# Interleaving the first two chunks of an FFT-and-MLP kernel, and moving the conversion of its second weight matrix

## The chip, the cores and the metric

The kernel runs on one core of one Trainium2 chip. The metric is the device time of one execution in microseconds (us). The engines are TensorE (PE, matrix products; PEld is its weight load), VectorE (DVE), ScalarE (ACT), GpSimd (POOL) and SyncE (SP, which issues most DMAs). Each engine runs its instructions in order; they wait for each other by semaphores.

## The reference

```python
def _attn_ref(x):                       # x: 8 x 3136 x 256
    X = np.fft.fft(x, axis=1)
    X = np.fft.fft(X, axis=2)
    return X.real.astype(np.float32)

def _moe_ref(x, g_ln, w_ch1, w_ch2):    # w_ch1: 256 x 1024, w_ch2: 1024 x 256
    mu = np.mean(x, axis=-1, keepdims=True)
    var = np.mean((x - mu) ** 2, axis=-1, keepdims=True)
    xn = (x - mu) / np.sqrt(var + 1e-06) * g_ln
    ch = np.maximum(xn @ w_ch1, 0.0) @ w_ch2
    return (x + ch).astype(np.float32)
```

The weights arrive as 64-bit floats, and the kernel converts them itself.

## The kernel before

**Stages.** The DFT over the 3136 rows of each of the 8 batches is split in two. `step1(b, i)` makes the inner transform of two of 14 row slices; its result goes to DRAM (`store1`) and comes back in another layout (`relayout`, tile `s2`). `step2(m, part)` makes the outer one for pair `m` of frequency groups (8 pairs for each batch, m counts over all). Its result in PSUM (`ps2`, one bank with the tag "fft" and one with the tag "y") is copied out as chunks of 256 tokens: `ckh` and `ckl`, a rounded part and the rest of it ("h" and "l" of `part`), and `ck`, the whole ("f").

**The MLP.** Every product in float32 is made as three products of rounded parts (`PASSES`). Only half of the frequencies is computed: a sum and a difference of two halves, `pa` and `pb`, give a token and its mirror. The work of a chunk is eight tiles, one for each 128 hidden features `f`. `s` numbers the tiles over all chunks: before, `c, f = divmod(s, 8)`. For a tile, `moe1_a(s)` is the first product (6 matmuls into `ab`, two buffers), ScalarE's copy `asb` and VectorE's two halves of `h`; `moe1_b(s)` is ScalarE's `h_hi` (ReLU and rounding) and VectorE's `h_lo`; `moe2(s)` is the second product, 12 matmuls into `acc`. `acc` of chunk c has the two banks of the tag `acc{c % 2}`. A first product can start only when `h` of the tile two before is made, since that empties its `ab`.

**Residual and end of a chunk.** `residual(c, i)` makes the reference's x again for 128 tokens (4 matmuls for both i, tile `psy`), before in the two banks of the other parity, `acc{(c + 1) % 2}`; `residual_e` (ScalarE, `ye`) and `residual_y` (VectorE, `y`, mean and variance) follow. `std` (ScalarE) and `inverse_std` (VectorE, `ve`, `r`) give the factor, `finish(c, i)` (VectorE, `o`) adds both parts, which empties `acc`; `store_out` writes.

**Weights.** Each quarter of w1 and of w2 is converted by `convert_z` (ScalarE, `ew`), `convert_m` (VectorE, `mw`, `fw`), `convert_b` (VectorE, `ew` twice) and, for w2, `finish_w2` (VectorE, `fw`). `split_w2` gives `w_hi` on ScalarE and `w_lo` on POOL. w1 is also transformed (`transform_w1`), rounded and its rest kept (`rest_w1`, `rest_w1_copy`: `w_lo`), in halves k: k=0 for f up to 3, k=1 from f=4. Quarter n of w2 serves f = 2n and 2n + 1.

**Order.** The order of PE, ACT, DVE and POOL is that in which the code is written; for SP too in the first part. A hand-written start runs to tile 5. Then a loop over s issues, for each step s: `moe1_b(s - 1)`, `moe1_a(s)`, the list `late[s]`, `moe2(s - 3)`, the list `after[s]`. `add_late` and `add` fill the lists: here stand the residuals, the ends of chunks, step1, step2 and the folds of later batches on POOL.

Of the kernel before, what the change touches and what calls it, by code (L numbers as in the profile page):

```python
# [146 lines left out]
def tile_kernel(ctx: ExitStack, tc: tile.TileContext, x, g_ln, w1, w2, tu, tab, tz, ty, tw, out):  # L147
# [192 lines left out]
    hh = {}  # L340

    def moe1_a(s, passes=((0, 1), (1, 0), (0, 0))):
        c, f = divmod(s, 8)
        w = width(c)
# [51 lines left out]
    def moe2(s, halves=((0, 0), (0, 1), (1, 0), (1, 1))):  # L396

        c, f = divmod(s, 8)
        hs = hh[s]
# [102 lines left out]
    def convert_a(key, wp):  # L502
        convert_m(key, wp)
        convert_z(key, wp)
# [181 lines left out]
    with tc.manual_schedule(engines={E.PE, E.Activation, E.DVE, E.Pool}):  # L686
        with tc.manual_schedule(engines={E.SP}):
# [61 lines left out]
            relayout(0, 0, 2)  # L749
            relayout(0, 2, 4)  # L750
            relayout(0, 4, 8)
            nc.sync.dma_start(tab_s[:, :, gb[4]:gb[8]], tab[:, :, gb[4]:gb[8]])
            load_w2(2)
            relayout(0, 8, 16)
# [9 lines left out]
            for i in range(NU):  # L764
# [31 lines left out]
            step2(1, "f")  # L796
            convert_a("w2_2", w2p[2])
            step2(1, "hl", 1)
            moe2(0)
            moe1_b(3)  # L800
            moe1_a(4)
            convert_b("w2_2")
            f = finish_w2(2)
            nc.gpsimd.tensor_scalar(out=neg, in0=ty_s[:, 1, 129:130], scalar1=2.0, scalar2=-1.0,
                                    op0=ALU.mult, op1=ALU.add)
            moe2(1)
            step2(2, "m")
            moe1_b(4)
            split_w2(2, f)
            moe1_a(5)  # L810
            step2(2, "hf")
            step2(2, "l")
            convert_a("w2_3", w2p[3])
# [41 lines left out]
```

## Time and profile before

| | us |
|---|---|
| median of 3 runs | 988.58 (988.18 to 991.56) |
| the profiled execution | 988.67 |
| its span | 986.9 |
| granted TensorE clock | 1.00 |

| engine | busy us | share of the span |
|---|---|---|
| PE | 976.8 | 99% |
| DVE | 815.5 | 83% |
| ACT | 535.6 | 54% |
| POOL | 252.1 | 26% |

The profile gives times in us from the span's start. A row of a timeline has start, duration, engine, line, operation, tiles written and read, and in brackets how long the engine stood idle before it and what ended that. Matmuls are pipelined: the duration of one is longer than the distance to the next. The chain is the work that ended last, followed back; its shares tell what the span consists of.

### The profile page before, as it was taken

Reading aid. Unit: us, or ns where it says so; the run is one execution under the profiler, and the core shown is the slowest. Engines: PE = TensorE matmul, PEld = TensorE weight load, DVE = VectorE, ACT = ScalarE, POOL = GpSimd, SP = SyncE. Lnnn points to the kernel's source line nnn. Section 1 sums busy time; section 2 is a strip of 40 time slices with the busy share of each in tenths; the row PEclk is TensorE's granted clock in tenths of the full one; section 3 lists DMA queues with packets and bytes.
Section 4 is the critical chain, followed back from the end, with each engine's and each line's share of the span. In section 5 each row is a group of like instructions: output and inputs, shape, how many; then the busy total and the mean of one; then the engine's idle time right before and its main releaser. Section 6 shows DMA issues by size and latency. Waiting matters only on the chain.

```text
span 986.9 us, 22042 instructions
## 1 busy us (share of the span) xinstructions
PE 976.8 (99%) x8426; PEld 962.9 (98%) x8427; DVE 815.5 (83%) x2190; ACT 535.6 (54%) x1416; POOL 252.1 (26%) x282
## 2 busy tenths in 40 slices
PE   9899999999999999999999999999999999999998
PEld 6699999999999999999999999999999999999998
DVE  6888887888888888878888888888888888888887
ACT  3655655555555555555555556555555554555553
POOL 3247343224322332322342234223322300000000
PEclk9999999999999999999999999999999999999999
DMA  8924352215221252112521242212311112100101
GB/s 336 330 101 134 101 173 76 87 54 150 76 97 55 75 161 87 65 65 73 164 86 54 86 139 87 96 55 75 109 52 36 54 53 88 44 23 22 44 23 44
DMA packets 41161, 92.12 MB, mean 93 GB/s; under 512 B 4080, under 2 KB 18400, under 8 KB 40160
## 3 DMA queue, kind: packets, MB, share of 16 engines
q1 hardware_dynamic: 39088, 87.25, 26.7%
q0 software_dynamic: 736, 2.47, 0.7%
q8 instruction: 67, 1.10, 0.5%
q10 hardware_dynamic: 1232, 0.99, 0.3%
q14 instruction: 38, 0.31, 0.1%
HBM read 50.32 MB, written 40.37 MB: 92 GB/s over the span
## 4 chain that ended last, share of the span: by engine, by line
PE 91%; DVE 7%; ACT 2%; issue 1%; ACTq 0%; DVEq 0%
PE acc L406 50%; PE ab L356 25%; PE ps L311 6%; PE psy L431 4%; PE ps L263 3%; DVE h_lo L371 2%; DVE h L362 1%; DVE h L363 1%; PE pw L683 1%; ACT h_hi L370 1%; DVE ew L538 0%; PE ps L255 0%; PE ps L257 0%; DVE fw L525 0%; DVE st L453 0%
## 5 line engine op out<-in xcount | busy, mean ns | idle before, releaser
L406 PE MATMUL acc<-w_hi,h_lo 128*128 128x256 f32 x1568 | 433.2, 276 | 0.2 <-DVE h_lo L371 0.2
L406 PE MATMUL acc<-w_hi,h_hi 128*128 128x256 f32 x1568 | 433.0, 276 | 0.0
L406 PE MATMUL acc<-w_lo,h_hi 128*128 128x256 f32 x1568 | 433.0, 276 | 0.0
L371 DVE SCALAR_TENSOR_TENSOR h_lo<-h,h_hi 128x512 fp32r<-128x512 f32 x392 | 294.1, 750 | 141.2 <-ACT h_hi L370 138.8
L370 ACT ACTIVATE h_hi<-h 128x512 fp32r<-128x512 f32 x392 | 250.0, 638 | 292.9 <-DVE h L363 292.9
L406 PEld LDWEIGHTS acc<-w_hi,h_lo 128*128 128x128 f32 x1568 | 294.3, 188 | 0.6 <-DVE h_lo L371 0.4
L406 PEld LDWEIGHTS acc<-w_hi,h_hi 128*128 128x128 f32 x1568 | 294.4, 188 | 0.0
L406 PEld LDWEIGHTS acc<-w_lo,h_hi 128*128 128x128 f32 x1568 | 294.4, 188 | 0.0
L356 PE MATMUL ab<-ckl,w_hi 128*128 128x256 f32 x768 | 218.0, 284 | 2.3 <-DVE h L363 2.3
L356 PE MATMUL ab<-ckh,w_lo 128*128 128x256 f32 x768 | 212.7, 277 | 2.0 <-ACT w_lo L594 1.7
L356 PE MATMUL ab<-ckh,w_hi 128*128 128x256 f32 x768 | 212.1, 276 | 0.0
L225 POOL TENSOR_TENSOR fl<-f,fh 128x512 fp32r<-128x512 f32 x49 | 64.0, 1306 | 504.9 <-ACT fh L219 494.2
L362 DVE TENSOR_TENSOR h<-asb,ab 128x256 f32<-128x256 f32 x384 | 158.7, 413 | 0.5 <-ACT asb L361 0.5
L363 DVE TENSOR_TENSOR h<-asb,ab 128x256 f32<-128x256 f32 x384 | 158.9, 414 | 0.0
L356 PEld LDWEIGHTS ab<-ckl,w_hi 128*128 128x128 f32 x768 | 144.2, 188 | 3.5 <-issue 1.9
L356 PEld LDWEIGHTS ab<-ckh,w_lo 128*128 128x128 f32 x768 | 144.3, 188 | 2.5 <-ACT w_lo L594 1.9
L356 PEld LDWEIGHTS ab<-ckh,w_hi 128*128 128x128 f32 x768 | 144.2, 188 | 0.0
L361 ACT COPY asb<-ab 128x256 f32<-128x256 f32 x384 | 137.9, 359 | 8.9 <-PE ab L356 1.2
L267 ACT COPY s<-ps 128x508 f32<-128x508 f32 x56 | 32.8, 586 | 62.6 <-PE ps L263 50.7
L311 PE MATMUL ps<-tab_s,s 112*128 112x98 f32 (+1 forms) x512 | 65.6, 273 | 0.1
L311 PEld LDWEIGHTS ps<-tab_s,s 112*128 112x128 f32 x512 | 61.8, 191 | 0.6 <-PE pw L683 0.6
L332 ACT CAST ckh<-ps 128x392 fp32r<-128x392 f32 (+49 forms) x112 | 39.7, 356 | 39.7 <-PE ps L311 39.5
(111 smaller groups left out, 980.2 us busy)
## 6 DMA issues: line engine op xcount, KB each, us to landing
xs<-x SPq DMA_DIRECT2D x56, 512.0 KB, 4.1
out<-o SPq DMA_DIRECT2D x96, 256.0 KB, 2.0
scratch<-s SPq DMA_DIRECT2D x49, 256.0 KB, 2.3
s<-scratch SPq DMA_DIRECT2D x7, 1792.0 KB, 9.8
w1p_all<-w SPq DMA_DIRECT2D x6, 512.0 KB, 8.9
scratch<-s POOLq DMA_DIRECT2D x4, 256.0 KB, 6.0
w1p_all<-w POOLq DMA_DIRECT2D x2, 512.0 KB, 5.2
s<-scratch SPq DMA_DIRECT2D x1, 896.0 KB, 10.9
```

The lines of the kernel that those rows point to most:

```text
L225: nc.gpsimd.tensor_tensor(out=lo, in0=f, in1=hi.bitcast(F32), op=ALU.subtract)
L267: nc.scalar.copy(s[:, :, :, :127], ps[:, :, :, :127])
L311: nc.tensor.matmul(ps[:, h, k0 - base:k1 - base], s2[b][:KP, g, 128 * h:128 * h + 128], tab_s[:, h, k0:k1], start=(h == 0 and g == 2 * j), ...
L332: nc.scalar.copy(hi, src)
L356: nc.tensor.matmul(pt, wt[wi][:, j, fs], ch[xi][:, j, :w], start=(n == 0), stop=(n == 2))
L361: nc.scalar.copy(asb[:, :w], pa)
L362: nc.vector.tensor_tensor(out=h[:, :w], in0=asb[:, :w], in1=pb, op=ALU.add)
L363: nc.vector.tensor_tensor(out=h[:, w:], in0=asb[:, :m], in1=pb[:, :m], op=ALU.subtract)
L370: nc.scalar.activation(h_hi, h, AF.Relu)
L371: nc.vector.scalar_tensor_tensor(out=h_lo, in0=h, scalar=0.0, in1=h_hi.bitcast(F32), op0=ALU.max, op1=ALU.subtract)
L406: nc.tensor.matmul(acc[c, i][:, side], hs[xi][:, h0:h0 + 128], ws[wi][:, f], start=(f == 0 and side == 0 and n == 0), stop=(f == 7 and n = ...
L431: nc.tensor.matmul(ps[:, j, :n], ck[:, j], ty_s[:, j, :n], start=(j == 0), stop=True, skip_group_check=True)
```

## The change

It makes five edits, all in the first 22 of the loop's steps and in the written start.

- The tiles of the first two chunks are taken in another order: four of chunk 0, three of chunk 1, the other four of chunk 0, the other five of chunk 1. `tile_of(s)` gives chunk and feature.
- `step2(2)` and the parts of the second chunk come earlier, behind tile 3; `rest_w1_copy(1)` comes later.
- The conversions of w2: quarters 0 and 1 earlier, `convert_m` of quarter 2 too; the rest of quarters 2 and 3 goes into the steps 6 to 10 of the loop. `load_w2(2)` goes ahead of `relayout(0, 4, 8)`.
- `residual(0, i)` comes in step 9 instead of 6, and in the banks "fft" and "y"; `residual(1, i)` in step 15 instead of 14, in acc0 as before.
- The end of chunk 0 comes in steps 14 and 15 (before 11 and 12), that of chunk 1 in 20 and 21 (before 19 and 20).

```diff
+    order = [(0, f) for f in range(4)] + [(1, f) for f in range(3)]
+    order += [(0, f) for f in range(4, 8)] + [(1, f) for f in range(3, 8)]
+    def tile_of(s):
+        return order[s] if s < 16 else divmod(s, 8)
...
     def residual(c, i):
-        ps = psum.tile([128, 2, 130], F32, tag="y" if i > 1 else f"acc{(c + 1) % 2}",
-                       name=f"psy{c}_{i}", bufs=1 if i > 1 else 2)
+        tag = "y" if i > 1 else ("fft", "y")[i] if c == 0 else f"acc{(c + 1) % 2}"
+        ps = psum.tile([128, 2, 130], F32, tag=tag, name=f"psy{c}_{i}",
+                       bufs=2 if tag[0] == "a" else 1)
...
     for c in range(LC):
-        s = 8 * c + (5 if c > 1 else 6)
-        add_late(8 * c + 9 + (c < 2), std, c)
-        add_late(8 * c + 10 + (c < 2), inverse_std, c)
+        s = (9, 15)[c] if c < 2 else 8 * c + 5
+        end = (14, 20)[c] if c < 2 else 8 * c + 11
+        add_late(end - 1 if c < 2 else end - 2, std, c)
+        add_late(end if c < 2 else end - 1, inverse_std, c)
         for i in range(2):
             add(s, residual, c, i)
             add_late(s + 1, residual_e, c, i)
             add_late(s + i + 2, residual_y, c, i)
-            add_late(8 * c + 11 + i, finish, c, i)
-            add(8 * c + 11 + i, store_out, c, i)
+            add_late(end + i, finish, c, i)
+            add(end + i, store_out, c, i)
...
             relayout(0, 2, 4)
+            load_w2(2)
             relayout(0, 4, 8)
             nc.sync.dma_start(tab_s[:, :, gb[4]:gb[8]], tab[:, :, gb[4]:gb[8]])
-            load_w2(2)
...
             rest_w1_copy(0)
+            convert_z("w2_0", w2p[0])
             transform_w1(1, 1)
             round_w1(1)
-            convert_z("w2_0", w2p[0])
             convert_m("w2_0", w2p[0])
             convert_b("w2_0")
-            split_w2(0, finish_w2(0))
+            f = finish_w2(0)
+            convert_z("w2_1", w2p[1])
+            split_w2(0, f)
             convert_m("w2_1", w2p[1])
+            convert_b("w2_1")
+            f = finish_w2(1)
...
-            convert_z("w2_1", w2p[1])
-            convert_b("w2_1")
+            split_w2(1, f)
+            convert_m("w2_2", w2p[2])
...
             moe1_a(2)
-            f = finish_w2(1)
             moe1_b(1)
-            split_w2(1, f)
+            step2(1, "hl", 1)
+            moe1_a(3)
+            step2(2, "m")
+            step2(1, "f")
+            step2(2, "h")
             moe1_b(2)
-            moe1_a(3)
+            moe2(0)
+            step2(2, "l")
+            moe1_b(3)
+            moe2(1)
+            step2(2, "f")
+            moe1_a(4)
             rest_w1_copy(1)
...
+            convert_z("w2_2", w2p[2])
...
             moe1_a(5)
             moe2(2)
-            add_late(6, convert_b, "w2_3")
-            add_late(6, lambda: w2f.append(finish_w2(3)))
-            add_late(7, lambda: split_w2(3, w2f.pop()))
+            add_late(6, convert_b, "w2_2")
+            add_late(7, lambda: w2f.append(finish_w2(2)))
+            add_late(7, lambda: split_w2(2, w2f.pop()))
+            add_late(8, convert_a, "w2_3", w2p[3])
+            add_late(9, convert_b, "w2_3")
+            add_late(10, lambda: w2f.append(finish_w2(3)))
+            add_late(10, lambda: split_w2(3, w2f.pop()))
```

How the instructions then stand is shown at three places. The number behind `h`, `asb`, `h_hi`, `ab` is the tile, that behind `psy`, `o`, `acc`, `ck` the chunk and the half. The lines of the changed file are some lines further on than those of the file before (first product 363 for 356, second 413 for 406, residual 439 for 431, h_hi 377 for 370, h_lo 378 for 371).

ScalarE (ACT) where it splits quarter 2 of w2. Before:

```order
L370 ACTIVATE h_hi3_445<-h3_415 128x512
L361 COPY asb4_456<-ab4_449 128x256
L370 ACTIVATE h_hi4_485<-h4_457 128x512
L542 CAST w2_hi_73<-fw2_2_425 128x512
L361 COPY asb5_498<-ab5_491 128x256
```

and of the change, with VectorE (DVE) at the same place behind it:

```order
L377 ACTIVATE h_hi6_547<-h6_529 128x512
L368 COPY asb7_558<-ab7_551 128x256
L550 CAST w2_hi_73<-fw2_2_357 128x512
L377 ACTIVATE h_hi7_580<-h7_559 128x512
L368 COPY asb8_591<-ab8_584 128x256
```

```order
L369 TENSOR_TENSOR h7_559<-asb7_558,ab7_551 128x256
L370 TENSOR_TENSOR h7_559<-asb7_558,ab7_551 128x256
L606 SCALAR_TENSOR_TENSOR fw2_2_357<-fw2_2_357,ew2_2_355 128x512
L378 SCALAR_TENSOR_TENSOR h_lo7_581<-h7_559,h_hi7_580 128x512
L369 TENSOR_TENSOR h8_592<-asb8_591,ab8_584 128x256
```

Before, w2_hi stood behind the h_hi of its step; now it stands ahead of h_hi7, and the fw that it reads stands behind h7 on VectorE. Quarter 3 stands in the same way ahead of h_hi10.

VectorE at the end of chunk 0. Before, where the two finishes stand:

```order
L474 SCALAR_TENSOR_TENSOR r0_729<-ve0_661 128x2
L480 SCALAR_TENSOR_TENSOR o0_0_731<-acc0_0_431,r0_729,y0_0_617 128x256
L482 SCALAR_TENSOR_TENSOR o0_0_731<-acc0_0_431,r0_729,y0_0_617 128x256
L371 SCALAR_TENSOR_TENSOR h_lo11_751<-h11_722,h_hi11_750 128x512
L362 TENSOR_TENSOR h12_762<-asb12_761,ab12_754 128x256
L363 TENSOR_TENSOR h12_762<-asb12_761,ab12_754 128x256
L480 SCALAR_TENSOR_TENSOR o0_1_766<-acc0_1_438,r0_729,y0_1_655 128x256
L482 SCALAR_TENSOR_TENSOR o0_1_766<-acc0_1_438,r0_729,y0_1_655 128x256
```

and of the change:

```order
L482 SCALAR_TENSOR_TENSOR r0_840<-ve0_754 128x2
L488 SCALAR_TENSOR_TENSOR o0_0_842<-acc0_0_438,r0_840,y0_0_712 128x256
L490 SCALAR_TENSOR_TENSOR o0_0_842<-acc0_0_438,r0_840,y0_0_712 128x256
L551 TENSOR_TENSOR t1_lo_79<-tu_s_80,t1_hi_78 128x128
L378 SCALAR_TENSOR_TENSOR h_lo14_862<-h14_831,h_hi14_861 128x512
L369 TENSOR_TENSOR h15_873<-asb15_872,ab15_865 128x256
L370 TENSOR_TENSOR h15_873<-asb15_872,ab15_865 128x256
L488 SCALAR_TENSOR_TENSOR o0_1_877<-acc0_1_445,r0_840,y0_1_748 128x256
L490 SCALAR_TENSOR_TENSOR o0_1_877<-acc0_1_445,r0_840,y0_1_748 128x256
```

The finishes of chunk 0 moved from h11 and h12 behind h14 and h15; ckl of pair 3, `ve` and `r` stand ahead of the first of them.

TensorE (PE) at the residual of chunk 1, which writes to the banks that these finishes empty. Before, between the second product of tile 11 and the first of tile 15:

```order
L406 MATMUL acc1_1_741<-w2_hi_73,h_hi11_750 128x256
L431 MATMUL psy1_0_865<-ty_s_85,ck1_344 128x129
L431 MATMUL psy1_0_865<-ty_s_85,ck1_344 128x130
L431 MATMUL psy1_1_868<-ty_s_85,ck1_344 128x129
L431 MATMUL psy1_1_868<-ty_s_85,ck1_344 128x130
L356 MATMUL ab15_875<-ckl1_346,w1_hi_76 128x256
```

and of the change, between the second product of tile 12 and the first of tile 16 (`pse` is the small product of the ends):

```order
L413 MATMUL acc1_1_573<-w2_hi_73,h_hi12_774 128x256
L237 MATMUL pse0_1_894<-e0c1_614,tu_s_80 128x14
L238 MATMUL pse0_1_894<-e0c1_614,tu_s_80 128x14
L241 MATMUL pse0_1_894<-one_90,masked_89 112x1
L439 MATMUL psy1_0_906<-ty_s_85,ck1_348 128x129
L439 MATMUL psy1_0_906<-ty_s_85,ck1_348 128x130
L439 MATMUL psy1_1_909<-ty_s_85,ck1_348 128x129
L439 MATMUL psy1_1_909<-ty_s_85,ck1_348 128x130
L363 MATMUL ab16_916<-ckl2_429,w1_hi_76 128x256
```

Before, two steps lay between the second finish (step 12) and this residual (step 14); now both stand in step 15.

More of the change, by code (lines that the diff above doesn't have):

```diff
@@ L340, in tile_kernel @@
     hh = {}
+    order = [(0, f) for f in range(4)] + [(1, f) for f in range(3)]
+    order += [(0, f) for f in range(4, 8)] + [(1, f) for f in range(3, 8)]
+    def tile_of(s):
+        return order[s] if s < 16 else divmod(s, 8)
     def moe1_a(s, passes=((0, 1), (1, 0), (0, 0))):
-        c, f = divmod(s, 8)
+        c, f = tile_of(s)
         w = width(c)
@@ L396, in moe2 @@
     def moe2(s, halves=((0, 0), (0, 1), (1, 0), (1, 1))):
-        c, f = divmod(s, 8)
+        c, f = tile_of(s)
         hs = hh[s]
@@ L789, in tile_kernel @@
             moe1_a(2)
-            f = finish_w2(1)
             moe1_b(1)
-            split_w2(1, f)
-            moe1_b(2)
-            moe1_a(3)
-            rest_w1_copy(1)
[L796 to L803, printed above, removed]
+            step2(1, "hl", 1)
[3 more added lines that the diff above has]
+            step2(2, "h")
+            moe1_b(2)
+            moe2(0)
[4 more added lines that the diff above has]
+            moe1_a(4)
+            rest_w1_copy(1)
+            convert_z("w2_2", w2p[2])
             nc.gpsimd.tensor_scalar(out=neg, in0=ty_s[:, 1, 129:130], scalar1=2.0, scalar2=-1.0,
                                     op0=ALU.mult, op1=ALU.add)
-            moe2(1)
-            step2(2, "m")
             moe1_b(4)
-            split_w2(2, f)
             moe1_a(5)
-            step2(2, "hf")
-            step2(2, "l")
-            convert_a("w2_3", w2p[3])
             moe2(2)
-            add_late(6, convert_b, "w2_3")
-            add_late(6, lambda: w2f.append(finish_w2(3)))
-            add_late(7, lambda: split_w2(3, w2f.pop()))
+            add_late(6, convert_b, "w2_2")
[5 more added lines that the diff above has]
+            add_late(10, lambda: split_w2(3, w2f.pop()))
             add_late(14, split, t1_hi, t1_lo, tu_s[:, 0:128])
```

## The prediction

> **What bounds the kernel now.** I read the page first, then TensorE's own timeline and the table of waits for the first 90 us, then VectorE's timeline over the same stretch.
>
> ```profile
> span 986.9 us, 22042 instructions
> PE 976.8 (99%) x8426; PEld 962.9 (98%) x8427; DVE 815.5 (83%) x2190; ACT 535.6 (54%) x1416; POOL 252.1 (26%) x282
> PE 91%; DVE 7%; ACT 2%; issue 1%; ACTq 0%; DVEq 0%
> ```
>
> TensorE is the bound: 91% of the chain. The change touches only the first 90 us, so the question is how much TensorE loses there, and when it reaches a point behind which nothing differs.
>
> ```profile
> 33.97 0.39 PE L356 MATMUL ab<-ckh,w_lo 128*128 128x256 f32 x1 [0.35 <-ACT ckh L332]
> 36.48 0.36 PE L356 MATMUL ab<-ckl,w_hi 128*128 128x256 f32 x1 [0.32 <-DVE h L363]
> 41.25 0.39 PE L356 MATMUL ab<-ckh,w_lo 128*128 128x256 f32 x1 [1.68 <-ACT w_lo L594]
> 73.25 0.37 PE L356 MATMUL ab<-ckl,w_hi 128*128 128x256 f32 x1
> 82.53 0.36 PE L356 MATMUL ab<-ckl,w_hi 128*128 128x256 f32 x1 [0.18 <-DVE h L363]
> 85.36 0.28 PE L356 MATMUL ab<-ckl,w_hi 128*128 128x256 f32 x1
> ...
> PE ab L356 <- DVE h L363: 2.3, 6, 0.8
> ```
>
> These are first products, and behind the dots one row of the table of waits: tile 0 starts at 33.97, tile 2 at 36.48, tile 4 at 41.25 after 1.68 us for w1_lo, tile 16 at 73.25, tile 20 at 82.53, tile 21 at 85.36. Six waits for VectorE's h add 2.3 us. With the starts after a wait (some 0.1 to 0.2 us each), TensorE loses about 7 us between 31 and 86 us. By tile 16 both programs have given TensorE the same work (first products 0 to 15, second products 0 to 12, both residuals, step2(0) to step2(3), the small matmuls of the ends). So tile 16 is the milestone, and tile 21 the check.
>
> ```profile
> 83.48 1.36 PE acc L406 x12
> ...
> 85.52 0.68 PE ab L356 x6
> ...
> 87.56 1.76 PE ps L311 x16
> 89.32 0.92 PE psy L431 x8
> ```
>
> A tile costs TensorE 0.68 + 1.36 = 2.04 us; step2 of one pair of groups costs 0.88 (half of the row of 1.76), a residual 0.92. Now VectorE, one tile without other work:
>
> ```profile
> 61.11 0.68 DVE L371 SCALAR_TENSOR_TENSOR h_lo<-h,h_hi 128x512 fp32r<-128x512 f32 x1
> 61.71 0.41 DVE L362 TENSOR_TENSOR h<-asb,ab 128x256 f32<-128x256 f32 x1
> 62.04 0.41 DVE L363 TENSOR_TENSOR h<-asb,ab 128x256 f32<-128x256 f32 x1
> 63.15 0.69 DVE L371 SCALAR_TENSOR_TENSOR h_lo<-h,h_hi 128x512 fp32r<-128x512 f32 x1 [0.70 <-ACT h_hi L370]
> 63.76 0.41 DVE L362 TENSOR_TENSOR h<-asb,ab 128x256 f32<-128x256 f32 x1
> ```
>
> From h to h 61.71 to 63.76, 2.05 us: 1.26 of VectorE's own (0.60 for h_lo, 0.33 for each half of h) and a gap in which ScalarE makes h_hi. Work put into the gap is free up to 0.78; beyond that the tile costs 1.26 plus that work. So VectorE with ScalarE has TensorE's pace and no reserve: it catches up only while TensorE does other things. The prices of what is put in:
>
> ```profile
> 49.41 0.42 DVE L523 TENSOR_SCALAR mw<-w1p_all 128x512 int32<-128x512 int32 x1
> ...
> 50.54 0.68 DVE L371 SCALAR_TENSOR_TENSOR h_lo<-h,h_hi 128x512 fp32r<-128x512 f32 x1
> ...
> 51.81 0.42 DVE L536 TENSOR_SCALAR ew<-ew 128x512 int32<-128x512 int32 x1
> ...
> 52.99 0.69 DVE L598 SCALAR_TENSOR_TENSOR fw<-fw,ew 128x512 f32<-128x512 f32 x1
> ...
> 57.06 0.28 DVE L445 TENSOR_TENSOR y<-ye,psy 128x129 f32<-128x129 f32 x1
> ...
> 58.13 1.13 DVE L371 SCALAR_TENSOR_TENSOR h_lo<-h,h_hi 128x512 fp32r<-128x512 f32 x1
> ...
> 59.85 0.28 DVE L445 TENSOR_TENSOR y<-ye,psy 128x129 f32<-128x129 f32 x1
> ...
> 64.42 0.16 DVE L470 RECIPROCAL ve<-ve 128x2 f32<-128x2 f32 x1
> ...
> 65.20 0.48 DVE L480 SCALAR_TENSOR_TENSOR o<-acc,r,y 128x256 f32<-128x256 f32 x1
> ...
> 66.00 0.68 DVE L371 SCALAR_TENSOR_TENSOR h_lo<-h,h_hi 128x512 fp32r<-128x512 f32 x1
> ...
> 72.07 0.62 DVE L336 TENSOR_TENSOR ckl<-ps,ckh 128x362 fp32r<-128x362 f32 x2
> ...
> 72.85 0.69 DVE L371 SCALAR_TENSOR_TENSOR h_lo<-h,h_hi 128x512 fp32r<-128x512 f32 x1
> ```
>
> Start to start: mw and fw (convert_m) 1.13, the pair ew (convert_b) 1.18, fw of finish_w2 0.69, y of i=0 1.07, y of i=1 with ve 1.26 (59.85 to 61.11), rstd 0.78, one finish 0.80, the two ckl with t_lo 0.78.
>
> **The change part by part.** *w2_0 and w2_1 converted earlier.* This goes into idle time (rows of VectorE, of SyncE's queue, of the DMA issues, and of the windows: busy us of the five engines, clock, DMA share, GB/s):
>
> ```profile
> 30.37 0.43 DVE L536 TENSOR_SCALAR ew<-ew 128x512 int32<-128x512 int32 x1 [2.10 <-ACT ew L531]
> ...
> 26.91 0.69 SPq L752 DMA_DIRECT2D tab_s<-tab  x1
> ...
> tab_s<-tab SPq DMA_DIRECT2D x1, 343.0 KB, 7.6
> ...
> 38.00:42.00 4.00, 2.32 (x19) 2.05 (x19) 3.38 (x6) 3.11 (x9) 1.87 (x2) 1.00 1.04 319
> ```
>
> VectorE stood 2.10 us idle at 28 to 30 us, and the second conversion (1.13 + 1.18 + 0.69 = 3.0 us) is done by about 33, when ckl is due. TensorE gains nothing by it at once: tile 0 still waits for step2 and its casts (the 0.35 at 33.97). *w2_2's load ahead of the relayout of groups 4 to 7 and of tab, on SyncE's queue.* tab lands at 26.91 + 7.6 = 34.5; 512 KB more ahead of it, at the 319 GB/s of the window, is 1.6 us: 36.1. step2(2) now stands behind tile 3, at about 37.9, so I cost it at nothing (without that cover, up to 1.6).
>
> *The new order.* Tile 4 is now the first of the second chunk and needs only the lower half of w1_lo, so the 1.68 us go (1.84 with the start). Tiles 2 and 3 from 36.5 (1.36), step2(2) (0.88), two second products (2.72): tile 4 starts at 41.4. Before, it started at 41.25 with step2(2) and one of these second products still to come (2.24), so TensorE is 2.1 us ahead.
>
> *VectorE then decides.* ScalarE takes tile 4's asb at about 42.3 (its six matmuls are over), then the two w_lo casts (1.08) and z of w2_2 (0.6, an array as large as w_hi's) ahead of h_hi:
>
> ```profile
> 40.60 1.08 ACT L594 CAST w_lo<-psw 128x512 fp32r<-128x512 f32 x2
> ...
> 53.71 0.62 ACT L542 CAST w_hi<-fw 128x512 fp32r<-128x512 f32 x1
> ```
>
> With asb's own 0.3 and 0.70 for h_hi and its hand-overs (the idle at 63.15), h_lo of tile 4 starts at about 44.9 and h of tile 5, 0.60 behind it, at 45.4. From there, tile by tile: h6 2.05 later (47.5); h7 1.26 + 1.18 (49.9). For h8 finish_w2(2) and split_w2(2) stand in the same step: w2_hi stands ahead of h_hi7 on ScalarE and waits for fw, which stands behind h7 on VectorE. The gap is fw 0.69, w_hi 0.62 and h_hi 0.70, less some 0.1 by which neighbours overlap: 1.9 instead of 0.78, so 3.2 us. Then POOL comes in:
>
> ```profile
> 39.99 1.27 POOL L543 TENSOR_TENSOR w_lo<-fw,w_hi 128x512 fp32r<-128x512 f32 x1 [5.54 <-ACT w_hi L542]
> 66.03 1.78 POOL L225 TENSOR_TENSOR fl<-f,fh 128x512 fp32r<-128x512 f32 x1 [4.90 <-ACT fh L219]
> ...
> 40.48 1.33 DVE L371 SCALAR_TENSOR_TENSOR h_lo<-h,h_hi 128x512 fp32r<-128x512 f32 x1 [0.61 <-ACT h_hi L370]
> ```
>
> POOL's w_lo starts when w_hi ends, h_lo 0.7 us later; the h_lo at 40.48 met a w_lo half done and took 1.33 instead of 0.69. The bounds of this collision are 0 (the h_lo at 66.00 began first and took 0.68, and POOL's fl took 1.78) and 0.64; POOL begins first here, so 0.64. The Trainium skill ("SBUF — State Buffer", Who interferes with whom) says that a VectorE instruction with two SBUF inputs and a reading GpSimd instruction lock each other out, whichever starts first keeping the port to its end. By it both collisions here are certain; by the mean of the two rows they would be half, and the sum 0.64 us lower.
>
> So h8 is 3.8 later (53.7). h9: 1.26 + 1.13 (56.1); h10: 1.26 + 1.18 (58.5); h11 3.8 again (finish_w2(3), split_w2(3)): 62.3; h12: 1.26 + 1.07 (64.6); h13: 1.26 + 1.26 (67.1); h14 2.05 (69.2). In step 14 now stand ckl with t_lo, rstd and the first finish: 1.26 + 0.78 + 1.58, so h15 at 72.8. Behind h15 (0.66) stands the second finish (0.80).
>
> *The residual of chunk 1.* It takes the two acc0 banks that these finishes empty, and stands on TensorE in the step of the second one (before: two steps later). TensorE has its own work done by about 71 and waits for the second finish until 72.8 + 0.66 + 0.80 + 0.1 = 74.4; behind it half a residual, 0.46, so tile 16 starts at 74.8. That is 1.55 us later than 73.25. VectorE has no arrears then, so the 0.35 us before tile 20 (0.18 idle and a slow start) go: +1.2. Other collisions with POOL (four h_lo, 0 to 0.64 each, as the 1.13 at 58.13) I take at 0.3 in all more than before. Residual 2 also moves next to its finish, but step2(4) and step2(5) (1.76) stand between: 0, up to 0.7.
>
> Sum: +1.5 us. The profiled execution took 988.67 us around its span of 986.9, 0.09 over the median: 990.2, against the median 990.1.
>
> **The rivals.** (1) The tail doesn't bind: VectorE's fillers fit better (no collisions, w2_hi hidden), and the second finish is done when TensorE gets there. Then tile 16 follows h13 and h14 alone, at about 71.6: -1.65 and -0.35, 986.6. For it: which of VectorE and POOL starts first is a matter of 0.1 us. Against it: the order on ScalarE leaves no way around w2_hi. (2) TensorE alone decides: from 41.4, twelve first products (8.16), eleven second (14.96), two residuals (1.84), step2 (0.88) and the ends (0.56) are 26.4 us, tile 16 at 67.8: -5.45 and -0.35, 982.8. It needs VectorE 6.6 us faster over eleven tiles; nothing shown gives that. (3) Slower: the wait at the residual of chunk 1 grows to some 6 us because all four further collisions occur (+2.6) and residual 2 waits (+0.7): 993.6. It decides when VectorE's second finish ends after 77. (4) The clock: in the window from 38 to 42 us TensorE stood 1.7 us and was granted 1.00. If the wait here, 1.4 and 1.9 us with 0.46 between, made the clock fall to half for as long again, that would cost up to 3.3: 993.5. The Trainium skill ("TensorE: Matmul & The Clock Gate", What's actually happening) puts an idle window of about 3.4 us before the clock halves; by that the wait is just too short. That the change doesn't do what it says is excluded: the program's order has every move.
>
> **How the numbers follow.** Likeliest is the sum: 0.60, with its own range 988.7 to 992.0. Rival 1 0.18, rival 2 0.06, rival 3 0.10, rival 4 0.03, the rest scattered. A measurement here tells about 0.5% (4.9 us) from no change, so faster means below 983.6 (rival 2 and a little: 0.07), slower above 993.5 (half of rivals 3 and 4 and a rest: 0.09), the same 0.84. The range takes rival 1 and stops short of 2 and 4: 986.0 to 993.2.
>
> **What would show it.** Right: no wait for w_lo at tile 4, which starts near 41.4; two h_hi of ScalarE, for tiles 7 and 10, behind w_hi with VectorE idle about 1.3 us; TensorE's longest wait, 1.5 to 3.5 us in two pieces, at the residual's matmuls near 71 to 74, released by VectorE's finish; tile 21 at 86 to 88 instead of 85.36; the granted clock 1.00. Wrong: no wait at that residual, or tile 21 before 84.5. What would make the prediction wrong is a VectorE order that I priced too high at steps 7 and 10.

## The result, and the profile after

The changed kernel takes 998.72 us (median of 6 runs, 997.77 to 1001.31), the kernel before 988.67 beside it: 1.0099 times as long, with an interval of [1.0081, 1.0116]. Forecast was 990.1, between 986.0 and 993.2. So it became 10 us slower where 1.5 us had been expected. One execution of run e10 below took 1022.68 us, some 27 us longer than the longest of its other five, and is left out of that run's figures.

The profiled execution took 1001.31 us, the longest of the six and 2.6 more than the median; its span is 999.5 us, against 986.9 in the kernel before. From its page:

```profile
PE 981.9 (98%) x8426; PEld 967.7 (97%) x8427; DVE 819.9 (82%) x2190; ACT 535.5 (54%) x1416; POOL 250.8 (25%) x282
...
PE 89%; DVE 6%; DMA 3%; ACT 1%; issue 1%; SPq 0%; POOL 0%; ACTq 0%; DVEq 0%; POOLq 0%
```

The number of matmuls is the same (8426), but they are busy 5 us longer, and the chain holds less of TensorE (89% instead of 91%) and 3% of DMA. Where it happens, TensorE's timeline shows:

```profile
34.80 0.39 PE L363 MATMUL ab<-ckh,w_lo 128*128 128x256 f32 x1 [0.35 <-ACT ckh L332]
...
36.19 0.39 PE L363 MATMUL ab<-ckl,w_hi 128*128 128x256 f32 x1 [0.89 <-DVE ckl L336]
...
38.98 0.36 PE L363 MATMUL ab<-ckl,w_hi 128*128 128x256 f32 x1 [0.91 <-DVE h L370]
...
44.78 0.39 PE L363 MATMUL ab<-ckl,w_hi 128*128 128x256 f32 x1 [0.43 <-DVE ckl L336]
...
66.04 0.39 PE L413 MATMUL acc<-w_lo,h_hi 128*128 128x256 f32 x1 [0.95 <-POOL w_lo L551]
...
77.38 0.71 PE L439 MATMUL psy<-ty_s,ck 128*128 128x129 f32 x4 [1.62 <-DVE o L490]
80.92 1.23 PE L439 MATMUL psy<-ty_s,ck 128*128 128x129 f32 x4 [2.83 <-DVE o L490]
81.80 0.57 PE L363 MATMUL ab<-ckl,w_hi 128*128 128x256 f32 x1
...
96.17 0.28 PE L363 MATMUL ab<-ckl,w_hi 128*128 128x256 f32 x1
```

Tile 4 (44.78) no longer waits for w_lo, but comes 3.4 us later than the 41.4 of the prediction. Chunk 1's residual waits 1.62 and 2.83 us for the two finishes. Tile 16 (81.80) is 8.55 us behind the 73.25 of before, tile 21 (96.17) 10.8 us behind 85.36. So 10.8 of the 12.6 us by which this span is longer are there by tile 21; the rest is taken up further down. TensorE also stands 0.95 us for the last w_lo of w2 (66.04), a wait that the kernel before does not have; VectorE has no gap from 65.21 to 72.8, so this wait is not what makes h late.

The first matmul of tile 16 takes 0.57 us instead of 0.37, which is the clock. The windows from 76.62 to 90.27 us, cut where the clock changes (busy us of the five engines, then PEclk, DMA share, GB/s):

```profile
76.62:80.03 3.41, 0.71 (x4) 0.52 (x4) 3.41 (x7) 0.17 (x1) 3.16 (x4) 1.00 0.20 77
80.03:83.45 3.42, 2.53 (x12) 2.53 (x13) 1.79 (x4) 0.63 (x1) 3.34 (x5) 0.50 0.20 77
83.45:86.86 3.41, 3.41 (x17) 3.41 (x17) 1.44 (x3) 1.76 (x6) 0.93 (x2) 0.50 0.00 0
86.86:90.27 3.41, 3.41 (x30) 3.41 (x30) 1.76 (x6) 1.34 (x3) 0.00 (x0) 1.00 0.02 5
```

Behind a stretch in which TensorE was busy for 0.71 of 3.41 us, the granted clock is half for 6.83 us, in which 2.53 + 3.41 = 5.94 us of work got done at half pace (the first products of tile 16 are 0.21 us apart, from 82.16 on, instead of some 0.12): 2.97 us lost.

Every wait marked here but those at 34.80 and 66.04 is for VectorE. VectorE at the start, at tiles 7 and 10 and in step 14:

```profile
31.58 0.43 DVE L531 TENSOR_SCALAR mw<-w1p_all 128x512 int32<-128x512 int32 x1 [0.53 <-DMA w1p_all<-w]
...
33.10 1.64 DVE L546 SCALAR_TENSOR_TENSOR ew<-w1p_all,ew 128x512 int32<-128x512 int32 x1
34.78 0.69 DVE L606 SCALAR_TENSOR_TENSOR fw<-fw,ew 128x512 f32<-128x512 f32 x1
...
36.57 1.59 DVE L533 SCALAR_TENSOR_TENSOR fw<-w1p_all,mw 128x512 f32<-128x512 uint32 x1
...
55.93 1.36 DVE L378 SCALAR_TENSOR_TENSOR h_lo<-h,h_hi 128x512 fp32r<-128x512 f32 x1 [1.22 <-ACT h_hi L377]
...
65.21 1.33 DVE L378 SCALAR_TENSOR_TENSOR h_lo<-h,h_hi 128x512 fp32r<-128x512 f32 x1 [1.22 <-ACT h_hi L377]
...
74.47 0.41 DVE L369 TENSOR_TENSOR h<-asb,ab 128x256 f32<-128x256 f32 x1
...
77.24 1.05 DVE L551 TENSOR_TENSOR t_lo<-tu_s,t_hi 128x128 fp32r<-128x128 f32 x1
78.21 1.21 DVE L378 SCALAR_TENSOR_TENSOR h_lo<-h,h_hi 128x512 fp32r<-128x512 f32 x1
79.34 0.41 DVE L369 TENSOR_TENSOR h<-asb,ab 128x256 f32<-128x256 f32 x1
```

And POOL at the same times:

```profile
32.91 1.29 POOL L551 TENSOR_TENSOR w_lo<-fw,w_hi 128x512 fp32r<-128x512 f32 x1 [7.93 <-ACT w_hi L550]
...
36.20 1.42 POOL L551 TENSOR_TENSOR w_lo<-fw,w_hi 128x512 fp32r<-128x512 f32 x1 [2.00 <-ACT w_hi L550]
...
76.87 1.27 POOL L225 TENSOR_TENSOR fl<-f,fh 128x512 fp32r<-128x512 f32 x1 [2.87 <-ACT fh L219]
78.10 0.77 POOL L213 TENSOR_TENSOR f<-zw 128x256 f32<-128x256 f32 x1
```

An ew (0.69 alone), an fw (0.69) and a t_lo (0.28 in the kernel before) that meet POOL take 1.64, 1.59 and 1.05 us.

### The profile page after: what moved, and what is told of

The parts are those of the page before. It is cut to its first block, busy times and chain, and to the rows that moved or that the text cites. A ratio compares the mean times of both kernels' runs of the same rounds, so it can differ in the third digit from the quotient of the medians.

```text
span 999.5 us, 22047 instructions
## 1 busy us (share of the span) xinstructions
PE 981.9 (98%) x8426; PEld 967.7 (97%) x8427; DVE 819.9 (82%) x2190; ACT 535.5 (54%) x1416; POOL 250.8 (25%) x282
## 4 chain that ended last, share of the span: by engine, by line
PE 89%; DVE 6%; DMA 3%; ACT 1%; issue 1%; SPq 0%; POOL 0%; ACTq 0%; DVEq 0%; POOLq 0%
PE acc L413 50%; PE ab L363 25%; PE ps L311 5%; PE psy L439 4%; PE ps L263 3%; DMA w1p_all<-w 3%; DVE h_lo L378 2%; DVE h L369 1%; DVE h L370 1%; ACT h_hi L377 1%; DVE ew L546 0%; DVE fw L533 0%; SPq L180 0%; DVE st L461 0%; ACT asb L368 0%
```

## The experiments

All are the changed kernel with edits, except e8, e10 and e11, which are the kernel before with one. In the diffs, `...` stands for lines or parts of lines left out. The expectations were written before each run and name theories by letters: A, the wait at chunk 1's residual and the clock behind it; B, VectorE's sum of work sets the pace, so that a wait taken away comes back elsewhere; C, the early conversions; D, the ping-pong of ScalarE and VectorE at tiles 7 and 10; E, the load that was moved ahead; F, the work piled into step 14. Medians in us, and the ratio to the kernel before with its interval:

| run | median | ratio |
|---|---|---|
| the change | 998.72 | 1.0099 [1.0081, 1.0116] |
| e1 residual of chunk 1 freed | 994.41 | 1.0061 [1.0049, 1.0073] |
| e2 conversions later | 998.16 | 1.0092 [1.0078, 1.0105] |
| e3 wait filled with matmuls | 996.36 | 1.0072 [1.0059, 1.0086] |
| e4 split_w2 later | 996.67 | 1.0079 [1.0063, 1.0095] |
| e5 = e1 + e2 | 994.20 | 1.0048 [1.0033, 1.0063] |
| e6 = e5 + load back | 994.07 | 1.0044 [1.0028, 1.0060] |
| e7 = e6 + finish_w2 earlier | 992.76 | 1.0034 [1.0019, 1.0049] |
| e8 before + load ahead | 988.61 | 0.9994 [0.9985, 1.0003] |
| e9 = e7 + three moves | 989.26 | 1.0005 [0.9995, 1.0015] |
| e10 before + the change's ends | 994.07 | 1.0050 [1.0037, 1.0063] |
| e11 before + w_lo earlier | 988.86 | 1.0004 [0.9995, 1.0012] |
| e12 = e9 + the end of chunk 1 earlier | 988.68 | 1.0001 [0.9993, 1.0010] |
| e13 only the ends mended | 992.84 | 1.0038 [1.0023, 1.0052] |
| e14 only the start mended | 995.29 | 1.0060 [1.0044, 1.0076] |
| e15 = e9, residual as in the change | 991.99 | 1.0029 [1.0018, 1.0040] |
| e16 = e12 with less work for VectorE | 987.02 | 0.9976 [0.9967, 0.9985] |

**The residual and the clock: e1 and e3.**

```diff
-        tag = ... else f"acc{(c + 1) % 2}"
+        tag = ... else "fft" if (c, i) == (1, 0) else f"acc{(c + 1) % 2}"
...
+            d = 1 if (c, i) == (1, 1) else 0
-            add(s, residual, c, i)
-            add_late(s + 1, residual_e, c, i)
+            add(s + d, residual, c, i)
+            add_late(s + d + 1, residual_e, c, i)
```

> After, with the first half of chunk 1's residual in the bank fft instead of acc0 and the second half one step later, so that neither waits for the second finish of chunk 0; all else as after. Theory A (the loss is the wait at this residual and the clock that falls behind it): the 4.75 us of waiting at the residual's matmuls go, of which some 1.4 us come back as a wait of tile 17 for h of tile 15 (79.34 in the trace of after); the granted clock stays near 1.00, which gives back 3.4 us more. 992, between 990 and 994. Theory B (VectorE sets the pace over the whole stretch, the residual is only where TensorE happens to meet it): the same microseconds turn up as waits for h at tiles 16 and 17, tile 21 stays near 96, and the time is within 2 us of 998.7.

e3 leaves the residual and puts matmuls ahead of each half:

```diff
+            if c == 1:
+                add(s, lambda n: warm_up(n, warm_h), (7, 12)[i])
             add(s, residual, c, i)
```

> After, with matmuls that compute nothing needed, put in ahead of each half of chunk 1's residual: 7 of them (about 1.5 us) into the wait of 1.76 us and 12 (about 2.6 us) into the wait of 3.00 us. The wait itself stays as long. Theory A: TensorE has no long gap there any more, the granted clock stays at 1.00, and the 3.4 us of half clock go: 995.3, between 994 and 996.5. If the slow pace of 118 ns per matmul behind the recovery belongs to the same event, up to 2 us more: 993.3. Rival (the clock fell for another reason, such as the power of all engines together in that stretch): the clock falls as in after and the time stays at 998.7 or a little above.

e3's TensorE:

```profile
75.55 1.69 PE L694 MATMUL pw<-warm_h 128*128 128x512 bf16 x6
77.12 0.71 PE L439 MATMUL psy<-ty_s,ck 128*128 128x129 f32 x4
77.67 2.75 PE L694 MATMUL pw<-warm_h 128*128 128x512 bf16 x12
80.67 0.71 PE L439 MATMUL psy<-ty_s,ck 128*128 128x129 f32 x4 [0.25 <-DVE o L490]
```

The halves start at 77.12 and 80.67, as late as in the change (77.38, 80.92), and the clock stayed at 1.00. It is 2.4 us faster (996.36 against 998.72). So theory A's half about the clock holds, at somewhat less than 3.4. e1 is 4.3 us faster, not the 6.7 that A promised. The mean granted clock was 1.00 in four of its five executions, and 0.996 or 0.997 in all six of the change. Part of what came back is in two waits of e1:

```profile
80.33 0.36 PE L363 MATMUL ab<-ckl,w_hi 128*128 128x256 f32 x1 [1.17 <-DVE h L370]
...
88.00 0.36 PE L413 MATMUL acc<-w_hi,h_lo 128*128 128x256 f32 x1 [1.08 <-DVE y L454]
```

Without the residual's wait TensorE stands 1.17 us for h of tile 15 and 1.08 us behind VectorE's y: theory B is right about that part. The profiled execution of e1 (995.82, 1.4 over its median) is the one with a mean clock of 0.998: behind the waits at its start it ran at half clock from 35.66 to 39.07. So the start, too, can bring the clock down.

**The start and the ping-pong: e2, e4 to e8.** e2 moves the conversions behind the work that TensorE waits for:

```diff
-            convert_b("w2_1")
-            f = finish_w2(1)
...
-            split_w2(1, f)
-            convert_m("w2_2", w2p[2])
+            convert_b("w2_1")
...
             moe1_a(2)
+            f = finish_w2(1)
             moe1_b(1)
+            split_w2(1, f)
...
             convert_z("w2_2", w2p[2])
+            convert_m("w2_2", w2p[2])
```

> After, with VectorE's part of the early conversions put back later: convert_b and finish_w2 of quarter 1 behind ckl and behind tile 2 (as in the kernel before), convert_m of quarter 2 beside its convert_z behind tile 4; the order of tiles as after. Theory C (the start is late because these five VectorE instructions stand ahead of ckl and of h of tile 0): tile 0 starts about 1 us earlier against its step2, the wait of 1.06 us at 37.6 goes, tile 4 starts some 2 us earlier than 44.78; if the later waits for VectorE don't eat it, 996 to 997. Theory B: the work has only moved, VectorE is as late at tile 15 as it was, and the time is 998 to 1000.

e4 puts the split of quarters 2 and 3 one step later:

```diff
-            add_late(7, lambda: split_w2(2, w2f.pop()))
+            add_late(8, lambda: split_w2(2, w2f.pop()))
...
-            add_late(10, lambda: split_w2(3, w2f.pop()))
+            add_late(11, lambda: split_w2(3, w2f.pop()))
```

> After, with split_w2 of quarters 2 and 3 one step later (steps 8 and 11), so that w_hi no longer stands on ScalarE ahead of h_hi while its source is still to be made on VectorE. Theory D (the ping-pong of ScalarE and VectorE at tiles 7 and 10 makes VectorE late for the second finish, 1.2 us of idling at each): VectorE gains about 2.4 us by tile 15, the wait at chunk 1's residual falls from 4.75 to about 2.4 us, and the clock stays at 1.00 since the longest piece is then under 2 us: 998.7 - 2.4 - 3.4 = 993. If the clock falls all the same, 996.3. Rival: w_lo on POOL collides with later VectorE instructions and nothing is gained: 998 to 999.

e5 is e1 and e2 together:

> The freed residual (first half of chunk 1's residual in the bank fft, second half one step later) together with the later conversions (convert_b and finish_w2 of quarter 1 behind ckl and tile 2, convert_m of quarter 2 behind tile 4). Without the fall of the clock at the residual the later conversions can be priced by themselves, against 994.4 of the freed residual alone. Theory C (VectorE's early work is what made the start late): tile 4 comes 0.7 us earlier behind step2(0), the drop of the clock near 36 us that the freed residual showed in one profile has less room, 993.0 to 993.8. Theory B (VectorE's sum of work decides): 994.2 to 994.8.

e6 also puts the load back:

```diff
-            load_w2(2)
             relayout(0, 4, 8)
             nc.sync.dma_start(tab_s[:, :, gb[4]:gb[8]], tab[:, :, gb[4]:gb[8]])
+            load_w2(2)
```

> As the kernel before it in this list, and load_w2 of quarter 2 is put back behind the load of tab. Theory E (the 512 KB ahead of the relayouts and of tab delay them by 0.5 to 1.5 us): the relayout of groups 0 and 1 lands near 30.6 us as in the kernel before, tab near 34.5 to 36, the wait of 0.5 us at step2(2) goes, and tile 4 comes at about 41.5 to 42. 992.3, between 991.5 and 993. Rival: the landings differ from run to run by as much, and nothing changes (993.5 to 994.5).

e7 also makes fw of quarters 2 and 3 one step earlier:

```diff
-            add_late(7, lambda: w2f.append(finish_w2(2)))
+            add_late(6, lambda: w2f.append(finish_w2(2)))
...
-            add_late(10, lambda: w2f.append(finish_w2(3)))
+            add_late(9, lambda: w2f.append(finish_w2(3)))
```

> As the kernel before it in this list, and finish_w2 of quarters 2 and 3 stands one step earlier (6 and 9), right behind convert_b, with split_w2 where it was: w_hi's source is then made a tile before ScalarE comes to it. Theory D (the ping-pong at tiles 7 and 10): VectorE no longer idles 1.2 us at each of the two h_lo, 1.2 us less at each: 990, between 989 and 991, near the kernel before. Rival: the collisions with POOL's w_lo stay or move to other instructions, 992.

e8, in the kernel before, moves the load alone (the reverse of e6's diff):

> The kernel before, with one part of the change alone: load_w2 of quarter 2 ahead of the relayout of groups 4 to 7 and of tab. Theory E: step2(0) starts 0.5 to 1.0 us later because its relayout shares the DMA engines with 512 KB more; tab's lateness is covered there, since step2(2) starts at 43.5; 989.3 to 989.8. Rival: within 0.2 of 988.7.

e2 gained 0.6 us, e5 0.2 over e1, e6 0.1 over e5; none is told from nothing. e8 is 0.9994 [0.9985, 1.0003]: ahead of the relayouts the load costs nothing, and theory E falls there. It does not try the other half, tab, since step2(2) comes at 43.5 in the kernel before. In e2, where step2(2) came at 38.14, TensorE waited 0.50 us for tab; in e5 it did not. step2(0), which waits for the relayout, started anywhere between 31.0 and 33.2 us in the executions profiled here, with the load in either place. e7 gained 1.3 us over e6 (D had 2.4), with spreads that overlap. e4 gained 2.0 with a wide spread (994.09 to 999.14): its residual waited 0.46 and 1.54 us instead of 1.62 and 2.83, nearly as D had it, but the clock fell all the same, twice in the profiled execution (from 65.67 and from 79.32). With the conversions and the load moved back, another wait stood ahead of tile 4, for ckl of the second chunk, here in e6:

```profile
43.24 0.38 PE L363 MATMUL ab<-ckl,w_hi 128*128 128x256 f32 x1 [1.50 <-DVE ckl L336]
```

This ckl stands on VectorE behind h_lo of tile 2, which waits for ScalarE.

**Step 14: e9, e10, e12.** e9 makes three moves in e7:

```diff
+            step2(2, "l")
             moe1_b(2)
             moe2(0)
-            step2(2, "l")
...
             moe1_a(5)
+            split(t1_hi, t1_lo, tu_s[:, 0:128])
-            add_late(14, split, t1_hi, t1_lo, tu_s[:, 0:128])
...
-        add_late(end if c < 2 else end - 1, inverse_std, c)
+        add_late(end if c == 1 else end - 1, inverse_std, c)
```

> The freed residual with the later conversions, the load back and finish_w2 a step earlier (992.8), and three more moves off VectorE's crowded places: step2(2)'s ckl ahead of h_lo of tile 2 (tile 4 waited 1.1 to 1.5 us for it), the split of the twiddle t_lo out of step 14 to behind tile 5, and chunk 0's inverse_std from step 14 to 13. Theory F (what is left of the loss is VectorE's work piled into step 14, 5.06 us from h of tile 14 to h of tile 15, and the ckl that tile 4 waits for): 5.06 falls to about 3.2, the wait of 1.2 us at tile 17 goes, tile 4 comes about 1 us earlier: 990.4, between 989.3 and 991.5. Rival (VectorE's whole sum decides, so that work moved out of step 14 is missing elsewhere): 992 to 993.

e10, in the kernel before:

```diff
-        s = 8 * c + (5 if c > 1 else 6)
-        add_late(8 * c + 9 + (c < 2), std, c)
-        add_late(8 * c + 10 + (c < 2), inverse_std, c)
+        s = (6, 15)[c] if c < 2 else 8 * c + 5
+        end = (14, 20)[c] if c < 2 else 8 * c + 11
+        add_late(end - 1 if c < 2 else end - 2, std, c)
+        add_late(end if c < 2 else end - 1, inverse_std, c)
...
-            add_late(8 * c + 11 + i, finish, c, i)
+            add_late(end + i, finish, c, i)
```

> The kernel before, with one part of the change alone: the end of chunk 0 in steps 14 and 15, that of chunk 1 in 20 and 21, and the residual of chunk 1 in step 15, still in acc0; order of tiles and conversions as before, residual 0 where it was. Theory A and F (the loss sits in the ends and the residual that were moved): tile 16 comes 2 to 4 us later than 73.25 because the residual waits for the second finish, perhaps with a fall of the clock: 992.5, between 991 and 995. Rival (the loss comes from the order of tiles and the conversions): 988.5 to 989.5.

e12, in e9:

```diff
-        end = (14, 20)[c] if c < 2 else 8 * c + 11
-        add_late(end - 1 if c < 2 else end - 2, std, c)
-        add_late(end if c == 1 else end - 1, inverse_std, c)
+        end = (14, 19)[c] if c < 2 else 8 * c + 11
+        add_late((end - 1, end)[c] if c < 2 else end - 2, std, c)
+        add_late((end - 1, end)[c] if c < 2 else end - 1, inverse_std, c)
```

> As the first kernel of this list, and the end of chunk 1 in steps 19 and 20 as in the kernel before (in the change: 20 and 21). Residual 2 in step 21 then no longer stands behind a finish of the same step: the way from tile 21 to tile 22 is 4.64 us as before instead of 5.19, if theory F is right 0.3 to 0.6 us better than the first kernel: 990.0. Rival: rstd and a finish in one step make h of tile 20 late by as much.

VectorE in e9, from h of tile 14 to h of tile 15:

```profile
70.49 0.41 DVE L369 TENSOR_TENSOR h<-asb,ab 128x256 f32<-128x256 f32 x1
...
72.48 0.68 DVE L378 SCALAR_TENSOR_TENSOR h_lo<-h,h_hi 128x512 fp32r<-128x512 f32 x1
73.08 0.41 DVE L369 TENSOR_TENSOR h<-asb,ab 128x256 f32<-128x256 f32 x1
```

That is 2.59 us instead of 4.87 (74.47 to 79.34): t_lo and r are elsewhere, and h_lo takes 0.68. e9 is 989.26, 3.5 us better than e7 and 1.1 better than expected; e12 is 988.68. Both are the kernel before again, within 0.2%. They keep the new order of tiles and the late end of chunk 0, so these by themselves cost nothing that shows. And e10, the change's ends alone, gives 5.4 us of loss. Its TensorE at the residual, and its windows:

```profile
73.15 0.71 PE L431 MATMUL psy<-ty_s,ck 128*128 128x129 f32 x4 [0.85 <-DVE o L482]
76.49 0.78 PE L431 MATMUL psy<-ty_s,ck 128*128 128x129 f32 x4 [2.62 <-DVE o L482]
```

```profile
39.46:42.87 3.41, 1.80 (x14) 1.73 (x15) 2.69 (x6) 3.41 (x10) 1.74 (x2) 1.00 1.07 319
73.59:77.01 3.42, 0.80 (x8) 0.60 (x6) 3.42 (x6) 0.63 (x1) 3.42 (x5) 1.00 0.20 77
77.01:80.42 3.41, 3.41 (x18) 3.41 (x17) 1.22 (x3) 1.72 (x6) 3.33 (x5) 0.50 0.20 77
```

So the ends bring the wait and the fall of the clock with the old order of tiles as well.

**Start and ends apart: e13, e14, e15.** e13 has of all these moves the freed residual, t_lo and inverse_std; e14 has those of e2, e6 and e7 and step2(2)'s ckl.

> After, with the ends alone mended: the freed residual of chunk 1, t_lo out of step 14, chunk 0's inverse_std in step 13; the written start and w2's conversions as in the change. The freed residual alone gave 994.4, both mended 989.3. Theory F (step 14 and the residual carry most): 991, and the rest of 2 us is the start. If the start carries as much as the ends: 993.5. If the start costs nothing behind VectorE's pace: 989.5.

> After, with the start alone mended: quarter 1's and 2's conversions later, the load back, finish_w2 a step earlier, step2(2)'s ckl ahead of h_lo of tile 2; the ends and the residual of chunk 1 as in the change. If the two parts add up, 998.7 - (what the start is worth by e13). Theory F: 996, with the wait at the residual's matmuls still there, 3.5 to 4.5 us, and the clock falling behind it. If being earlier at the start takes the wait away by itself: 992.

> As e9, with the residual of chunk 1 as in the change: both halves in acc0 and in step 15, behind both finishes. If the wait at it is only VectorE's lateness in step 14: a wait of 0.5 us or less, 989.5. If the banks as such make it (TensorE is through with its own work before any second finish can be done): e9 had h of tile 15 at 73.41 and the second finish done at 74.6, TensorE there at 71.9; so 2.5 us of waiting in two pieces, of which tile 17's own wait for h takes none back, 991.5; the clock falls in the executions in which one window of about 3.4 us holds most of it.

The four combinations are 998.72 (neither), 992.84 (ends mended), 995.29 (start mended), 989.26 (both). The ends are worth 5.9 or 6.0 us, the start 3.4 or 3.6: they add up, and "the start costs nothing behind VectorE's pace" falls. (The start here includes e7's move, in steps 6 and 9.) e15 differs from e9 in the residual of chunk 1 alone, and costs 2.7 us more, though VectorE is on time:

```profile
72.29 0.71 PE L439 MATMUL psy<-ty_s,ck 128*128 128x129 f32 x4 [0.59 <-DVE o L490]
74.34 0.71 PE L439 MATMUL psy<-ty_s,ck 128*128 128x129 f32 x4 [1.34 <-DVE o L490]
```

This is an execution at a mean clock of 1.00, of which there were two: 990.37 and 991.39. The other ten had 0.997 or 0.998 and took 991.02 to 994.97, so part of the 2.7 us may be the clock again; the runs do not settle how much.

**Where the 1.68 us went: e11 and e16.** e11 moves one line of the kernel before:

```diff
+            rest_w1_copy(1)
             split_w2(1, f)
             moe1_b(2)
             moe1_a(3)
-            rest_w1_copy(1)
```

> The kernel before, with the two w_lo casts of rest_w1_copy(1) put on ScalarE ahead of w_hi of quarter 1, into the 0.89 us in which ScalarE waits there for fw. It aims at the same 1.68 us in front of tile 4 that the change removes, by one move. If TensorE keeps what it gains: 987.2. If VectorE's pace takes it back at tiles 5 to 7, as theory B says: 988.2 to 988.8. It also takes away the one gap of the kernel before that is long enough for the clock to fall.

e16, in e12, leaves out two pairs of ew:

```diff
-            add_late(6, convert_b, "w2_2")
...
-            add_late(9, convert_b, "w2_3")
```

> As e12, with convert_b of quarters 2 and 3 of w2 left out: two pairs of ew on VectorE, 1.18 us each, in steps 6 and 9. The second half of w2 is then not the right one; the instructions behind it are the same and take the same time. Theory B (VectorE sets the pace from tile 5 to tile 20): what VectorE saves comes through to TensorE, 988.7 - 2.4 = 986.3, between 986 and 987.5. Rival (TensorE or a load sets the end of this stretch): 988.7.

In e11 the wait for w_lo is gone and tile 4 starts at 39.01 instead of 41.25 (0.4 of that was there at tile 0). Three waits follow, at tiles 6, 7 and 8:

```profile
39.01 0.28 PE L356 MATMUL ab<-ckl,w_hi 128*128 128x256 f32 x1
...
45.03 0.36 PE L356 MATMUL ab<-ckl,w_hi 128*128 128x256 f32 x1 [0.45 <-DVE h L363]
...
48.54 0.36 PE L356 MATMUL ab<-ckl,w_hi 128*128 128x256 f32 x1 [0.32 <-ACT ck L334]
...
51.71 0.35 PE L356 MATMUL ab<-ckl,w_hi 128*128 128x256 f32 x1 [0.88 <-DVE h L363]
```

The kernel before waits at the last of these alone:

```profile
52.03 0.36 PE L356 MATMUL ab<-ckl,w_hi 128*128 128x256 f32 x1 [0.29 <-DVE h L363]
```

So 0.45 + 0.32 + 0.59 = 1.36 us of waiting are new, and each wait is followed by a slow first matmul. At tile 8 (51.71 against 52.03) the gain is given back but for what was there at tile 0, and the time is 988.86. Two of the three waits are for VectorE, the 0.32 for ScalarE's ck. The gap of 1.68 us that e11's expectation calls long enough for the clock to fall did not make it fall in e10, which has it too (window 39.46 to 42.87 above). In e16 2.36 us less of VectorE's work give 1.7 us (987.02 against 988.68): VectorE is what decides up to tile 20. e16 leaves work out, so it is no version to use. None of the complete versions beats the kernel before.

## Why the prediction was wrong

The mechanisms that the prediction named came, at tiles 7 and 10 and at the residual. What failed are three terms: the conversions at the start (put at nothing, 3.4 us late by tile 4), VectorE's other collisions with POOL (put at 0.3 us, measured 3.1) and the clock (a rival with a chance of 0.03, 3.0 us in the profile).

- **"This goes into idle time"**, said of w2_0 and w2_1, and tile 4 at 41.4: it came at 44.78, 3.4 us late. The second conversion was done at 35.4, not at 33: its quarter landed at 31.5, and POOL's first w_lo (32.91 to 34.20) held an ew for 1 us. The collisions with POOL that I priced at tiles 7 and 10 I did not look for at the start. `convert_m` of quarter 2, ahead of h of tile 0, had no price in the sum at all; it met the second w_lo, and TensorE's wait for h at tile 2 was 0.91 us instead of 0.32. And "step2(2) now stands behind tile 3" counted TensorE alone, not the ckl between it and tile 4. Against the prediction's starts, of the 3.4 us 0.8 was there at tile 0, where step2(0) got its relayout at 32.22 instead of 31.36, which differs from execution to execution; the ckl made 1.05, h of tile 2 0.6, and the way from tile 2 to tile 4 0.9. The 3.4 to 3.6 us that e13 and e14 give the start hold e7's move as well, so that the two figures agree is in part chance.
- **"w2_2's load ahead ... at nothing"** came true, by luck in part. tab landed at 38.5 (issued at 27.46, 11.0 us to landing) and not at 36.1. step2(2) at the forecast 37.9 would have waited for it, as it did in e2; it came at 40.47 because the start was late.
- **VectorE's chain, tiles 7 and 10**: right. Both h_lo stand idle 1.22 us and take 1.36 and 1.33. The Trainium skill ("SBUF — State Buffer", Who interferes with whom) made both collisions certain; the trace agrees with it, and with the full 0.64 us.
- **"Other collisions with POOL ... 0.3 in all"**, and h15 at 72.8: the mis-sized term. h of tile 15 came at 79.34, 6.5 late. Of these, 3.5 had come down from the start (h of tile 8 at 57.22 instead of 53.7). Another 1.8 came in steps 8 to 13, where POOL ran nearly without a gap from 55.45 to 59.25 and from 64.72 to 74.00:

```profile
57.88 0.87 DVE L531 TENSOR_SCALAR mw<-w1p_all 128x512 int32<-128x512 int32 x1
58.85 0.94 DVE L533 SCALAR_TENSOR_TENSOR fw<-w1p_all,mw 128x512 f32<-128x512 uint32 x1
...
70.85 0.68 DVE L466 TENSOR_SCALAR ve<-mv 128x2 f32<-128x2 f32 x1
...
73.48 1.07 DVE L378 SCALAR_TENSOR_TENSOR h_lo<-h,h_hi 128x512 fp32r<-128x512 f32 x1 [0.70 <-ACT h_hi L377]
```

  In the kernel before these take 0.42, 0.69, 0.17 and, without POOL, 0.68; an h_lo at 68.19 took 0.89. That makes 1.8 us. The last 1.3 came in step 14, from h14 to h15, where 3.6 us were forecast and 4.87 came: t_lo took 1.05 instead of 0.28 and h_lo 1.21 instead of 0.69. Together 3.1 us. That POOL is the cause is read off rows that overlap; no run takes POOL's work away.
- **The residual of chunk 1**: the mechanism was right, the wait was 4.45 us instead of 3.3. e15 shows that even with VectorE on time its place costs 2.7 us of the median.
- **Rival 4, the clock**: given 0.03, and it happened in every run of the change (mean granted clock 0.996 or 0.997). I took the longest single gap (1.9 us) and the idle window that the prediction cites for the same thing. In the window behind which the clock fell TensorE was busy for 0.71 of 3.41 us, with two gaps in it; and e4 shows a fall behind gaps of about 1 us (below), so the longest single gap is not what decides. Rival 3's sign, a second finish that ends after 77, came too (80.9): the longer wait and the fall of the clock came together.
- **Residual 2, "0, up to 0.7"**: from tile 21 to tile 22 the changed kernel and e9 take 5.19 us, the kernel before 4.64 and e12 4.64: 0.55. In the median e12 gained 0.6 on e9, within the error of both.

Added up against the trace: tile 21 at 85.36 + 1.2 (forecast) + 3.4 (start) + 3.1 (VectorE up to tile 15) + 3.0 (clock) = 96.1; measured 96.17. Behind it the profiled execution loses 1.8 us more: 0.55 at residual 2, the rest while its matmuls run slower (last section).

Taking away the wait that the change aims at brings nothing by itself: in e11 one line does it and the time stays, since VectorE's and ScalarE's pace takes the gain back in four tiles.

## What to carry to other kernels

Before pulling work of a second engine forward into a wait of the first, ask what is late next on that second engine: where its own chain sets the pace, the wait only moves. Price collisions with POOL wherever a VectorE instruction is moved beside POOL's, also at places that were free of them; here instructions with one input were held up as well as those with two. Do not let a matmul take PSUM banks that another engine empties in the same step: here two waits close together cost themselves and then a stretch of half clock.

## What the runs showed of the hardware

- The clock falls for 3.41 us or twice that, and a gap need not be long. e4's clock fell at 65.67 behind a window whose longest gap was 0.96 us:

```profile
62.26:65.67 3.41, 1.93 (x12) 1.56 (x13) 3.25 (x9) 2.77 (x6) 1.92 (x2) 1.00 0.08 34
65.67:69.08 3.41, 3.41 (x19) 3.41 (x18) 3.31 (x9) 1.08 (x4) 3.41 (x5) 0.50 0.34 103
```

  Windows with 0.71, 0.80 and 1.93 of 3.41 us busy were followed by half clock, and so was e1's from 32.25 to 35.66 with 2.29, but e10's 39.46 to 42.87 with 1.80 was not; where the bound lies, and whether the kind of matmul counts, stays open. The Trainium skill ("TensorE: Matmul & The Clock Gate", What's actually happening) has a free-running window of 3413 ns; the lengths agree. If it runs free, the same waits can fall into one window or into two. e4's executions fit that (994.09 us at a mean clock of 0.998, 999.14 at 0.993), but no run here shows it.
- Beside POOL, VectorE instructions with one input took longer too: mw 0.87 us instead of 0.42, ve (128x2) 0.68 instead of 0.17. Not every overlap costs: the ve at 61.03 in the kernel before lay beside a POOL instruction and took 0.17.
- TensorE's matmuls are 4% slower for some 50 us behind the change's stretch of half clock, at a granted clock of 1.00 (busy us and count of PE first). What causes it is open; it is not the fall of the clock alone, since in e3, whose profiled execution had no such fall, second products stand 0.118 instead of 0.113 us apart between 99 and 117 us.

```profile
110.00:138.00 28.00, 28.00 (x241) 28.00 (x240) 23.25 (x65) 16.47 (x41) 10.92 (x14) 1.00 0.29 103
138.00:160.00 22.00, 22.00 (x197) 22.00 (x196) 17.23 (x48) 11.45 (x31) 8.45 (x10) 1.00 0.56 179
```

  241 in 28 us are 8.6 per us, 197 in 22 us 8.95.
